# Eighteen small loads that nothing reads, in the queue of a decode block's cache loads

## The chip, the cores and the metric

The kernel runs on one core of a Trainium2 chip. The metric is the device time of one execution in microseconds (us). Three runs of the kernel before took 1303.91, 1304.32 and 1304.37 us; their median is 1304.32 us. One more execution was recorded by the profiler, and everything that is said here of single instructions and transfers comes from that one.

## The reference

The kernel computes one decode step of a transformer block for a batch of 2 sequences, one new token each, in float32. The width is 448. Attention has 16 heads of 256 numbers and a cache of 8192 keys and values for each head; behind it stands a gated network of width 1792 without a nonlinearity.

```python
def _A_ref(x, k_cache, v_cache, wq, wo):
    q = (x @ wq).reshape(B, Sq, H, Dh).transpose(0, 2, 1, 3)
    scores = jnp.einsum("bhqd,bhkd->bhqk", q, k_cache) * (Dh ** -0.5)
    p = _softmax(scores, axis=-1)
    o = jnp.einsum("bhqk,bhkd->bhqd", p, v_cache)
    return o.transpose(0, 2, 1, 3).reshape(B, Sq, H * Dh) @ wo

def _B_ref(x, w_gate, w_up, w_down):
    return ((x @ w_gate) * (x @ w_up)) @ w_down

h = x + _A_ref(_layernorm(x), k_cache, v_cache, wq, wo)
h2 = h + _B_ref(_layernorm(h), w_gate, w_up, w_down)
```

There are 32 pairs of a head and a sequence. Each has 8 MB of keys and 8 MB of values (8192 x 256 numbers of 4 bytes), so the two caches are 512 MB of the 561 MB that the kernel reads.

## The kernel before

A pair of a head and a sequence is called a query here; the loop `for i in range(NQ)` goes over the 32 of them. For each query two transfers are issued on SyncE's queue (SP), one behind the other in the program: `load_k` (L98) fetches its keys into a tile of 128 rows with 64 KB each, and `load_v` (L103) its values into another tile of the same size. Both tiles come from pools: the pool of K has one buffer, that of V has two.

With the keys, TensorE (PE) forms the scores in PSUM (L253). In every third query VectorE (DVE) first multiplies and adds half of the keys itself (L241, L245), and PE only sums its result (L259). DVE finds the maximum (L319), ScalarE (ACT) forms the exponentials `p` (L323), and DVE multiplies them with the values and adds up: in one pair of instructions for eight rows of blocks (L338, L339) or in eight single instructions (L342). After the loop come the weights `wo` (L351), gate, up and down (L358) on the same queue, and the matmuls of the output projection and of the gated network.

What sets the order: the schedule is by hand (`manual_schedule`), so each engine runs its instructions as the program writes them. SyncE issues one transfer after the other, and a transfer that has to wait holds all those behind it on SyncE. K of the next query waits until the last reader of the one K buffer is done (the scores, or DVE's part of them), and for the load that filled it before. V waits until the query before the last one has been read out of its buffer. Once issued, a transfer's rows lie in the rings of the 16 DMA engines, which work them off in order; SyncE goes on without waiting for them to land. There are eight semaphores for the completions of transfers (DMAHW0 to DMAHW7), used in turn.

The tile pool `const` (one buffer for each name) holds small tiles that live to the end, such as `oacc`, `nm` and `qd`.

Of the kernel before, what the change touches and what calls it, by code (L numbers as in the profile page):

```python
# [8 lines left out]
F32 = mybir.dt.float32  # L9
# [6 lines left out]
P = 128  # L16
# [4 lines left out]
GK = SK // G  # L21
# [38 lines left out]
def tile_decode_block(  # L60
# [24 lines left out]
    nc = tc.nc  # L85
    const = ctx.enter_context(tc.tile_pool(name="const", bufs=1))
# [9 lines left out]
    def load_k(b, h):  # L96
        t = kbuf.tile([P, 2, G, GK], F32, tag="k", align_bytes=512, name=f"k_{h}_{b}")
        nc.sync.dma_start(t.rearrange("p c g k -> p (c g k)"), kc[b, h])  # L98
        return t

    def load_v(b, h):
        t = vbuf.tile([P, NO, GK], F32, tag="v", align_bytes=512, name=f"v_{h}_{b}")
        nc.sync.dma_start(t.rearrange("p o k -> p (o k)"), vc[b, h])  # L103
        return t
# [62 lines left out]
    for rows, c, to in LAYOUT:  # L167
        k = rows.stop - rows.start
        n = c.stop - c.start
# [58 lines left out]
    def queries(h):  # L228
        q = one.tile([P, 2, B, R], F32, tag="q", name=f"q_{h}")
        nc.scalar.activation(  # L230
            q.rearrange("p c b r -> p (c b) r"),
            qT.rearrange("p k g j c b -> p (k g j) (c b)")[:, h, :, None]
            .to_broadcast([P, 2 * B, R]),
            AF.Copy,
        )
        return q

    def scores(s, q, i, kt):
        upper = kt[:, 1]
        if by_vector(i):  # L240
            nc.vector.tensor_scalar(  # L241
                upper[:, 0], upper[:, 0], qd[:, 0, i : i + 1], None, op0=ALU.mult
            )
            for o in range(1, G):
                nc.vector.scalar_tensor_tensor(  # L245
                    upper[:, 0], upper[:, o], qd[:, o, i : i + 1], upper[:, 0],
                    op0=ALU.mult, op1=ALU.add,
                )
        tiles = [slice(j * MM, (j + 1) * MM) for j in range(GK // MM)]
        for at in tiles:  # L250
            for c in range(1 if by_vector(i) else 2):
                for g in range(G):
                    nc.tensor.matmul(  # L253
                        s[g * R : (g + 1) * R, at], q[:, c, i % B, :], kt[:, c, g, at],
                        start=(c == 0), stop=(c == 1), skip_group_check=True,
                    )
        if by_vector(i):
            for at in tiles:
                nc.tensor.matmul(  # L259
                    s[:, at], block, upper[:, 0, at], start=False, stop=True,  # L260
                    skip_group_check=True,
                )

    def weights(a, z):

        n = z - a
        nmT = ps_m.tile([n, P], F32, tag="sm", name=f"nmT_{a}")
        nc.tensor.transpose(nmT, nm[:, a:z], ident)
        low = work.tile([n, 1], F32, tag="low", name=f"low_{a}")
        nc.vector.tensor_reduce(low, nmT, axis=AX.X, op=ALU.min)  # L270
        diag = work.tile([n, n], F32, tag="diag", name=f"diag_{a}")
        nc.vector.tensor_scalar(diag, ident[:n, :n], low, None, op0=ALU.mult)
        all_ps = ps_m.tile([P, n], F32, tag="sm", name=f"all_ps_{a}")
        nc.tensor.matmul(all_ps, ones[:n, :], diag, start=True, stop=True)
        w = work.tile([P, n], F32, tag="w", name=f"w_{a}")
        nc.vector.scalar_tensor_tensor(
            w, all_ps, float(R), nm[:, a:z], op0=ALU.mult, op1=ALU.subtract
        )
        nc.scalar.activation(w, w, AF.Exp)
        lw = work.tile([P, n], F32, tag="lw", name=f"lw_{a}")  # L280
        nc.vector.tensor_mul(lw, ls[:, a:z], w)
        l_ps = ps_m.tile([P, n], F32, tag="sm", name=f"l_ps_{a}")
        nc.tensor.matmul(l_ps, ones, lw, start=True, stop=True)
        rl = work.tile([P, n], F32, tag="rl", name=f"rl_{a}")
        nc.vector.reciprocal(rl, l_ps)
        nc.vector.tensor_mul(w, w, rl)
        return w

    def weigh(a, z, w):
        nc.vector.tensor_mul(  # L290
            oacc[:, a:z], oacc[:, a:z], w[:, :, None].to_broadcast([P, z - a, NO])
        )

    def turn(a, z):
        oT_ps = ps_m.tile([P, z - a, 2], F32, tag="sm", name=f"oT_ps_{a}")
        for r in range(G):
            nc.tensor.matmul(
                oT_ps[r * R : (r + 1) * R], gsum, oacc[:, a:z, r::G], start=True, stop=True
            )
        return oT_ps  # L300

    def heads_out(a, z, oT_ps):
        nc.vector.tensor_copy(
            oT[:, a // B : z // B].rearrange("p h c b -> p h b c"),
            oT_ps.rearrange("p (h b) c -> p h b c", b=B),
        )

    q_now = queries(0)

    for i in range(NQ):  # L310
        h, b = divmod(i, B)
        kt = load_k(b, h)
        vt = load_v(b, h)

        s = ps_s.tile([P, GK], F32, tag="s", name=f"s_{i}")
        scores(s, q_now, i, kt)
        if i == EARLY:
            oT_ps = turn(0, EARLY)
        nc.vector.tensor_reduce(nm[:, i : i + 1], s, axis=AX.X, op=ALU.max, negate=True)  # L319
        if i == EARLY:  # L320
            heads_out(0, EARLY, oT_ps)
        p = one.tile([P, GK], F32, tag="p", name=f"p_{i}")
        nc.scalar.activation(  # L323
            p, s, AF.Exp, bias=nm[:, i : i + 1], scale=1.0, accum_out=ls[:, i : i + 1]
        )

        if b == B - 1 and h + 1 < H:
            q_now = queries(h + 1)

        if i == EARLY - 1:  # L330
            w = weights(0, EARLY)
        if i == NQ - 1:
            w = weights(EARLY, NQ)

        n = WIDE[i % 3] if i < EARLY - B else 0
        if n:
            v = vt[:, :n, :]
            nc.vector.tensor_mul(v, v, p[:, None, :].to_broadcast([P, n, GK]))  # L338
            nc.vector.tensor_reduce(oacc[:, i, :n], v, axis=AX.X, op=ALU.add)  # L339
        for o in range(n, NO):  # L340
            v = vt[:, o, :]
            nc.vector.scalar_tensor_tensor(  # L342
                v, v, 1.0, p, op0=ALU.mult, op1=ALU.mult, accum_out=oacc[:, i, o : o + 1]
            )
        if i == EARLY - 1:
            weigh(0, EARLY, w)
# [26 lines left out]
    for c in range(DC):  # L373
        k = P if c < DC - 1 else HALF
# [32 lines left out]
    for m in range(DC + 1):  # L407
        at = min(m, DC - 1)
        rows = slice(0, P) if m < DC - 1 else slice((m - at) * HALF, (m - at + 1) * HALF)
        k = rows.stop - rows.start  # L410
# [11 lines left out]
    for rows, c, to in LAYOUT:  # L422
        k = rows.stop - rows.start
# [23 lines left out]
    for half in range(2):  # L447
        at = slice(half * 2 * P, (half + 1) * 2 * P)
        nc.vector.tensor_mul(hm[:, at], u_ps[:, at], g_sb[:, at])  # L449
    for half in range(2):  # L450
        for n in range(2):
            k = (2 * half + n) * P
# [81 lines left out]
```

## Time and profile before

| | |
|---|---|
| runs of the kernel | 1303.91, 1304.32, 1304.37 us; median 1304.32 us |
| the profiled execution | 1304.25 us, of which the span from first to last instruction is 1302.4 us |
| busy, share of the span | PE 26%, DVE 81%, ACT 6% |
| bytes read | 561.19 MB, 431 GB/s over the span |
| DMA packets | 11401, of which 1266 have under 512 bytes |
| granted TensorE clock, mean | 0.646 |

The busy time of an engine is the time in which one of its instructions runs. A DMA packet is one piece that one DMA engine moves in one go; a row of a tile of K or V is one packet of 65536 bytes. A completion, the write that tells a semaphore that a DMA engine has done its share of a transfer, is a packet of its own too, of 4 bytes. The view that lists stretches counts for its DMA columns the packets that start in the stretch: their whole time as a share of 16 engines, and their bytes. In a stretch of 10 ns with one packet in it, the share times 16 times 10 ns is that packet's time.

### The profile page before, as it was taken

The numbers are of one execution on the slowest core, as the hardware profiler recorded it, in microseconds if no ns is written. First come the engines' busy times: TensorE is split into PE (matmuls) and PEld (weight loads), VectorE is DVE, ScalarE is ACT, GpSimd is POOL, SyncE is SP. The second block draws the span as 40 slices with busy tenths as digits, with TensorE's granted clock in tenths as the row PEclk, the third lists the DMA queues.
The fourth block names the chain that finished last, engine by engine and source line by source line (L and its number), as shares of the span: only waits on it lengthen the run. The fifth ranks groups of instructions, "written<-read, shape, count | busy, mean of one in ns | idle before, by whom it ended". The sixth has DMA issues, their size and how long they took to land.

```text
span 1302.4 us, 5013 instructions
## 1 busy us (share of the span) xinstructions
PE 342.4 (26%) x2116; PEld 101.8 (8%) x2116; DVE 1061.1 (81%) x381; ACT 74.3 (6%) x89; POOL 1.4 (0%) x12
## 2 busy tenths in 40 slices
PE   2432112222212322211222211223211222221147
PEld 0100000000000000000000000000000000000012
DVE  1499879969987998899799889969987996967743
ACT  0100000000000000000000000000000000000000
POOL 0000000000000000000000000000000000000000
PEclk9766566676557666656766656676656667655769
DMA  9999999999999999999999999999999999999998
GB/s 419 419 449 421 447 423 443 427 443 427 441 429 439 427 441 427 439 431 437 427 437 427 439 431 435 436 433 437 431 439 431 439 429 439 429 442 425 445 414 354
DMA packets 11401, 561.50 MB, mean 431 GB/s; under 512 B 1266, under 2 KB 1524, under 8 KB 2420
## 3 DMA queue, kind: packets, MB, share of 16 engines
q1 hardware_dynamic: 11380, 561.20, 99.6%
q8 instruction: 16, 0.26, 0.1%
q14 instruction: 5, 0.04, 0.0%
HBM read 561.19 MB, written 0.00 MB: 431 GB/s over the span
## 4 chain that ended last, share of the span: by engine, by line
DMA 71%; PE 19%; DVE 9%; issue 1%; SPq 0%; ACT 0%; DVEq 0%
DMA k<-in_kc_dram 68%; PE s L253 15%; DVE k L245 6%; PE s L259 3%; DMA gu_t<-in_B_w_up_dram 3%; DVE v L342 2%; DVE k L241 1%; PE ff_ps L460 0%; PE u_ps L187 0%; SPq L358 0%; SPq L351 0%; PE ff_ps L453 0%; DVE tail L449 0%; SPq L107 0%; ACT tail L465 0%
## 5 line engine op out<-in xcount | busy, mean ns | idle before, releaser
L253 PE MATMUL s<-k,q 128*32 128x512 f32 x1696 | 255.5, 767 | 875.7 <-DMA k<-in_kc_dram 875.7
L338 DVE TENSOR_TENSOR v<-v,p 128x16384 f32<-128x16384 f32 x19 | 327.3, 17226 | 68.8 <-DMA v<-in_vc_dram 49.1
L339 DVE TENSOR_REDUCE oacc<-v 128x8 f32<-128x16384 f32 x19 | 327.2, 17220 | 0.7
L342 DVE SCALAR_TENSOR_TENSOR v<-v,p 128x2048 f32<-128x2048 f32 x104 | 231.1, 2288 | 33.9 <-ACT p L323 21.9
L253 PEld LDWEIGHTS s<-k,q 128*32 128x32 f32 x1696 | 68.8, 137 | 1059.4 <-issue 1059.4
L323 ACT ACTIVATE p<-s,nm 128x2048 f32<-128x2048 f32 x32 | 63.0, 1967 | 1128.6 <-DVE nm L319 1128.6
L319 DVE TENSOR_REDUCE nm<-s 128x1 f32<-128x2048 f32 x32 | 73.1, 2285 | 65.1 <-PE s L259 43.2
L245 DVE SCALAR_TENSOR_TENSOR k<-k,qd 128x2048 f32<-128x2048 f32 x33 | 77.6, 2352 | 1.2
L259 PE MATMUL s<-k,block 128*128 128x512 f32 x88 | 42.1, 622 | 33.5 <-DVE k L245 33.5
L241 DVE TENSOR_SCALAR k<-k,qd 128x2048 f32<-128x2048 f32 x11 | 14.2, 1287 | 13.1 <-DMA k<-in_kc_dram 11.0
L259 PEld LDWEIGHTS s<-k,block 128*128 128x128 f32 x88 | 16.4, 196 | 60.0 <-DVE k L245 39.9
L159 DVE COPY xT<-wq_t 128x8 f32<-128x8 f32 x1 | 0.2, 173 | 18.9 <-DMA wq_t<-in_wq_dram 18.9
L385 PE MATMUL acc_ps<-wo_t,oT 128*2 128x448 f32 x64 | 9.8, 712 | 11.8 <-DMA wo_t<-in_wo_dram 11.5
L187 PE MATMUL q_ps<-wq_t,xr 128*32 128x512 f32 x64 | 8.9, 704 | 1.3 <-DVE xr L172 1.0
L211 DVE COPY qT<-q_ps 128x32 f32<-128x32 f32 x2 | 0.4, 192 | 10.5 <-PE q_ps L208 10.5
L342 DVE DVE_READ_ACCUMULATOR v<-v,p 128x1 f32 x104 | 8.7, 83 | 0.0
L323 ACT ACTIVATION_READ_ACCUMULATOR p<-s,nm 128x1 f32 x32 | 6.2, 193 | 0.0
L142 PE MATMUL total_x<-sum_h_x,ones 128*128 128x2 f32 x2 | 0.6, 364 | 21.1 <-DVE sum_h_x L135 21.1
L449 DVE TENSOR_TENSOR tail<-u_ps,tail 128x256 f32<-128x256 f32 x2 | 0.8, 420 | 6.1 <-PE u_ps L187 6.1
L460 PE MATMUL ff_ps<-wd_t,hmT 128*2 128x224 f32 x28 | 5.5, 352 | 0.0
L460 PE MATMUL acc_ps<-wd_t,hmT 128*2 128x224 f32 x28 | 5.5, 352 | 0.0
L230 ACT ACTIVATE q<-qT 128x128 f32<-128x128 f32 x16 | 4.8, 297 | 0.0
(94 smaller groups left out, 58.9 us busy)
## 6 DMA issues: line engine op xcount, KB each, us to landing
wq_t<-in_wq_dram SPq DMA_DIRECT2D x1, 7172.0 KB, 19.7
wo_t<-in_wo_dram SPq DMA_DIRECT2D x1, 3584.0 KB, 17.8
wo_t<-in_wo_dram SPq DMA_DIRECT2D x1, 2688.0 KB, 23.8
gu_t<-in_B_w_gate_dram SPq DMA_DIRECT2D x1, 1792.0 KB, 29.2
gu_t<-in_B_w_up_dram SPq DMA_DIRECT2D x1, 1792.0 KB, 35.8
wd_t<-in_wd_dram SPq DMA_DIRECT2D x2, 896.0 KB, 17.2
gu_t<-in_B_w_gate_dram SPq DMA_DIRECT2D x1, 1344.0 KB, 32.0
wo_t<-in_wo_dram SPq DMA_DIRECT2D x1, 896.0 KB, 25.5
```

Source lines behind the costliest of these rows:

```text
L187: nc.tensor.matmul(ps[32 * g : 32 * g + 32, : wide[g]], xs.rearrange("p b r -> p (b r)"), w[:, at : at + wide[g]], start=(c == 0), stop=(c ...
L241: nc.vector.tensor_scalar(upper[:, 0], upper[:, 0], qd[:, 0, i : i + 1], None, op0=ALU.mult)
L245: nc.vector.scalar_tensor_tensor(upper[:, 0], upper[:, o], qd[:, o, i : i + 1], upper[:, 0], op0=ALU.mult, op1=ALU.add,)
L253: nc.tensor.matmul(s[g * R : (g + 1) * R, at], q[:, c, i % B, :], kt[:, c, g, at], start=(c == 0), stop=(c == 1), skip_group_check=True,)
L259: nc.tensor.matmul(s[:, at], block, upper[:, 0, at], start=False, stop=True, skip_group_check=True,)
L319: nc.vector.tensor_reduce(nm[:, i : i + 1], s, axis=AX.X, op=ALU.max, negate=True)
L323: nc.scalar.activation(p, s, AF.Exp, bias=nm[:, i : i + 1], scale=1.0, accum_out=ls[:, i : i + 1])
L338: nc.vector.tensor_mul(v, v, p[:, None, :].to_broadcast([P, n, GK]))
L339: nc.vector.tensor_reduce(oacc[:, i, :n], v, axis=AX.X, op=ALU.add)
L342: nc.vector.scalar_tensor_tensor(v, v, 1.0, p, op0=ALU.mult, op1=ALU.mult, accum_out=oacc[:, i, o : o + 1])
L385: nc.tensor.matmul(acc_ps[32 * j : 32 * j + B, :], oT[:, h, c, :], wo_t[:, k * D : (k + 1) * D], start=(h < 2 and j > 0), stop=(h >= H - 2 ...
L460: nc.tensor.matmul(ps, hmT[:, n, g, :], wd_t[:, k * D + a : k * D + a + YC], start=False, stop=(k == NF - 1), skip_group_check=True,)
```

## The change

A tile `scratch` of 80 bytes a row is added to the pool `const`. Behind V of queries 4 to 21 a load is issued, 18 in all, that copies a few bytes from the first V of the cache into `scratch`. Nothing reads `scratch`. Each of the 18 has another size: `rulers` gives the first row, the number of rows, the step between rows and the number of runs in a row; the size in numbers of 4 bytes is 2 more than its place in the list. All are issued by SyncE.

```diff
+    rulers = (
+        (0, 3, 1, 1), (64, 3, 1, 1), (0, 3, 4, 1), (0, 16, 1, 1), (0, 17, 1, 1), (0, 32, 1, 1),
+        (0, 48, 1, 1), (0, 64, 1, 1), (64, 64, 1, 1), (0, 96, 1, 1), (0, 112, 1, 1),
+        (16, 112, 1, 1), (0, 119, 1, 1), (0, 120, 1, 1), (0, 124, 1, 1), (0, 125, 1, 1),
+        (0, 8, 1, 2), (0, 3, 1, 2),
+    )
+    scratch = const.tile([P, 20], F32, name="scratch")
+
+    def load_ruler(n):
+        at, rows, step, runs = rulers[n]
+        size = 2 + n
+        to = scratch[at : at + (rows - 1) * step + 1 : step, :size]
+        src = vc[0, 0, at : at + (rows - 1) * step + 1 : step]
+        if runs == 1:
+            nc.sync.dma_start(to, src[:, :size])
+        else:
+            half = size // 2
+            to = scratch[at : at + rows, :20].rearrange(
+                "p (k z) -> p k z", k=2
+            )[:, :, :half]
+            src = src[:, : 2 * GK].rearrange("p (k z) -> p k z", k=2)[:, :, :half]
+            nc.sync.dma_start(to, src)
+
     q_now = queries(0)
 
     for i in range(NQ):
         h, b = divmod(i, B)
         kt = load_k(b, h)
         vt = load_v(b, h)
+        if 4 <= i < 22:
+            load_ruler(i - 4)
```

The instructions of PE, DVE, ACT and GpSimd keep their order; SyncE's queue gets 18 transfers more. The first place is where they begin, on SyncE from K of query 4 (`k_2_0`, head 2, sequence 0) on. Before:

```order
L98 DMA k_2_0_356<-in_kc_dram 128x16384 [waits DMAHW7_49,DVE_49,PE_49]
L103 DMA v_2_0_358<-in_vc_dram 128x16384 [waits DMAHW6_49]
L98 DMA k_2_1_398<-in_kc_dram 128x16384 [waits DMAHW1_49,PE_49]
L103 DMA v_2_1_400<-in_vc_dram 128x16384 [waits DMAHW0_49,DVE_49]
L98 DMA k_3_0_448<-in_kc_dram 128x16384 [waits DMAHW3_49,PE_49]
L103 DMA v_3_0_450<-in_vc_dram 128x16384 [waits DMAHW2_49,DVE_49]
```

The same stretch of SyncE's queue now; in brackets stand the semaphores that a transfer waits for.

```order
L98 DMA k_2_0_357<-in_kc_dram 128x16384 [waits DMAHW7_49,DVE_49,PE_49]
L103 DMA v_2_0_359<-in_vc_dram 128x16384 [waits DMAHW6_49]
L323 DMA scratch_192<-in_vc_dram 3x2
L98 DMA k_2_1_400<-in_kc_dram 128x16384 [waits DMAHW1_49,PE_49]
L103 DMA v_2_1_402<-in_vc_dram 128x16384 [waits DMAHW0_49,DVE_49]
L323 DMA scratch_192<-in_vc_dram 3x3
L98 DMA k_3_0_451<-in_kc_dram 128x16384 [waits DMAHW4_49,PE_49]
L103 DMA v_3_0_453<-in_vc_dram 128x16384 [waits DMAHW2_49,DVE_49]
L323 DMA scratch_192<-in_vc_dram 3x4 [waits DMAHW3_49]
```

Each small load stands between V of its query and K of the next one. The third waits for the completion of the first (DMAHW3), since both write row 0 of `scratch`; K and V wait for the same partners as before, whose semaphores have other numbers.

The second place is SyncE's queue from V of query 7 (`v_3_1`) on, where the load of 17 rows stands. Before:

```order
L103 DMA v_3_1_484<-in_vc_dram 128x16384 [waits DMAHW4_49]
L98 DMA k_4_0_526<-in_kc_dram 128x16384 [waits DMAHW7_49,PE_49]
L103 DMA v_4_0_528<-in_vc_dram 128x16384 [waits DMAHW6_49,DVE_49]
L98 DMA k_4_1_574<-in_kc_dram 128x16384 [waits DMAHW1_49,PE_49]
L103 DMA v_4_1_576<-in_vc_dram 128x16384 [waits DMAHW0_49,DVE_49]
```

Now:

```order
L103 DMA v_3_1_488<-in_vc_dram 128x16384 [waits DMAHW5_49]
L323 DMA scratch_192<-in_vc_dram 16x5 [waits DMAHW1_49]
L98 DMA k_4_0_531<-in_kc_dram 128x16384 [waits DMAHW2_49,PE_49]
L103 DMA v_4_0_533<-in_vc_dram 128x16384 [waits DMAHW6_49,DMAHW0_49,DVE_49]
L323 DMA scratch_192<-in_vc_dram 17x6 [waits DMAHW4_49]
L98 DMA k_4_1_580<-in_kc_dram 128x16384 [waits DMAHW5_49,PE_49]
L103 DMA v_4_1_582<-in_vc_dram 128x16384 [waits DMAHW3_49,DVE_49]
```

A small load here waits for the small load before it (the one of 17 rows for that of 16, DMAHW4). V of query 8 has one wait more: its semaphore, DMAHW6, was last used by the second small load, three queries earlier.

## Rows read from the trace of the kernel before

**Rows 1.** The page: span, DMA shares in 40 slices, packets, bytes, the chain's lines.

```profile
span 1302.4 us, 5013 instructions
...
DMA  9999999999999999999999999999999999999998
...
DMA packets 11401, 561.50 MB, mean 431 GB/s; under 512 B 1266, under 2 KB 1524, under 8 KB 2420
...
HBM read 561.19 MB, written 0.00 MB: 431 GB/s over the span
...
DMA k<-in_kc_dram 68%; PE s L253 15%; DVE k L245 6%; PE s L259 3%; DMA gu_t<-in_B_w_up_dram 3%; DVE v L342 2%; DVE k L241 1%; PE ff_ps L460 0%; PE u_ps L187 0%; SPq L358 0%; SPq L351 0%; PE ff_ps L453 0%; DVE tail L449 0%; SPq L107 0%; ACT tail L465 0%
```

**Rows 2.** The chain in order of time: start us, us, what.

```profile
633.06 26.27 DMA k<-in_kc_dram
...
659.46 8.48 PE s L253 x64
667.96 30.02 DMA k<-in_kc_dram
...
707.76 28.84 DMA k<-in_kc_dram
...
1253.03 37.48 DMA gu_t<-in_B_w_up_dram
1290.55 1.05 PE u_ps L187 x6
```

**Rows 3.** SyncE's issues, 620 to 720 us: start us, us, what.

```profile
633.06 0.33 SPq L98 DMA_DIRECT2D k<-in_kc_dram  x1
633.44 0.42 SPq L103 DMA_DIRECT2D v<-in_vc_dram  x1
667.96 0.33 SPq L98 DMA_DIRECT2D k<-in_kc_dram  x1
674.62 0.33 SPq L103 DMA_DIRECT2D v<-in_vc_dram  x1
707.76 0.33 SPq L98 DMA_DIRECT2D k<-in_kc_dram  x1
713.48 0.33 SPq L103 DMA_DIRECT2D v<-in_vc_dram  x1
```

**Rows 4.** The tile v: its costliest form (min/median/max ns), issue to landing.

```profile
L342 DVE SCALAR_TENSOR_TENSOR v<-v,p x104: 2284/2289/2294, 137.8 to 1275.2; 128x2048 f32<-128x2048 f32 x104
...
DMA to landing us min/median/max: 42.3/42.8/58.3
```

**Rows 5.** Stretches, most of 10 ns with one DMA packet.

```profile
core 0: us, PE busy (x) PEld busy (x) DVE busy (x) ACT busy (x) POOL busy (x), PEclk, DMA share, GB/s
660.12:660.13 0.01, 0.01 (x4) 0.00 (x0) 0.01 (x1) 0.00 (x0) 0.00 (x0) 0.50 15.11 6554
1298.74:1298.75 0.01, 0.01 (x4) 0.00 (x0) 0.00 (x0) 0.00 (x0) 0.00 (x0) 1.00 0.46 179
676.59:676.60 0.01, 0.00 (x0) 0.00 (x0) 0.01 (x1) 0.00 (x0) 0.00 (x0) 0.50 0.06 0
316.77:316.78 0.01, 0.01 (x8) 0.01 (x3) 0.01 (x1) 0.00 (x0) 0.00 (x0) 1.00 5.92 1638
317.70:317.71 0.01, 0.01 (x4) 0.00 (x0) 0.01 (x1) 0.00 (x0) 0.00 (x0) 1.00 18.12 6554
600.00:1240.00 640.00, 149.26 (x893) 43.18 (x893) 540.15 (x194) 36.53 (x43) 0.00 (x0) 0.63 1.00 434
```

**Rows 6.** DMA packets of four stretches: 38.6:39.6, 1236.5:1238.4, 1238.4:1239.2, 1239.2:1240.2.

```profile
DMA packets 32, 1.05 MB, mean 1049 GB/s; under 512 B 16, under 2 KB 16, under 8 KB 16
...
DMA packets 25, 1.05 MB, mean 552 GB/s; under 512 B 9, under 2 KB 9, under 8 KB 9
...
DMA packets 2, 0.13 MB, mean 164 GB/s; under 512 B 0, under 2 KB 0, under 8 KB 0
...
DMA packets 19, 0.79 MB, mean 786 GB/s; under 512 B 7, under 2 KB 7, under 8 KB 7
```

## The prediction

> **What bounds the kernel now.** I read the page first: the DMA engines are at 9 tenths or more in 39 of 40 slices, and the chain of work that ended last is 68% waiting for K [rows 1]. Then the chain in order of time. K lands at 633.06 + 26.27 = 659.33, at 667.96 + 30.02 = 697.98 and at 707.76 + 28.84 = 736.60: one query every 38.64 us [rows 2]. A row of K or V is one packet of 65536 bytes, and it takes 15.11 x 16 x 10 ns = 2.418 us [rows 5]. A query has 256 of them, 16 for each of the 16 rings, and 16 x 2.418 = 38.69 us. So in mid-run a ring does nothing but such packets, one behind the other, and from 600 to 1240 us the share is 1.00 at 434 GB/s [rows 5].
>
> SyncE's issues show why no ring runs dry: K is issued at 707.76 while V, issued at 674.62, lands only 42.8 us later, at 717.4 [rows 3, 4]. K's issue waits for the scores, but the data are 8 to 10 us behind the queue. What an engine saves is worth nothing, and what a ring gets to do in addition comes on top, unless that ring had a lead.
>
> Some rings have one. The 16 completions of the first K lie within 1 us (38.6 to 39.6); those of the last K fall into 9 up to 1238.4, none up to 1239.2, and 7 after that [rows 6]. The seven late rings set the end, the nine others are roughly 1 to 3 us ahead. At the end the chain goes through the last transfer of `up`, 37.48 us, into the last matmuls [rows 2], so a late ring delays the end by its whole lag.
>
> **The change, part by part.** Nothing is removed. Added are 18 loads with 1080 rows or runs in all (1058 rows in the sixteen with one run, 2 x 8 and 2 x 3 in the other two).
>
> Bytes: under 60 KB in all, which at 434 GB/s is 0.14 us. I count it in the packets.
>
> SyncE: an issue takes 0.33 to 0.42 us [rows 3]. The small load stands behind V. V at 674.62 is issued by 674.95, and the small load before it lies behind the V of 633.44, which lands 42.8 us later at 676.2 [rows 3, 4]. So SyncE waits there 1 to 4 us (the rings that end last included) and issues the small load before about 680. What is queued behind it is K of the next query, and that isn't ready before 707.76. The cover is 27 us, and the cost nothing; were it gone, K's data still would not be missed for another 8. The extra wait of V of query 8 is for a load of three queries before: nothing.
>
> SBUF: `scratch` takes 80 bytes a row, and other tiles may move. DVE's instruction on V takes 2284 to 2294 ns in both V buffers [rows 4], so its place doesn't matter: nothing.
>
> Rings: this is the term. Each row is a small packet, and each ring that takes part adds a completion. No packet of 8 to 76 bytes stands in the trace, so I bound its price. Below: a completion of 4 bytes takes 0.06 x 16 x 10 ns = 9.6 ns [rows 5]. Above: a packet of 1792 bytes takes 0.46 x 16 x 10 ns = 74 ns, of which 66 ns are its bytes at the rate of the large ones (65536 bytes in 2418 ns), so 8 ns are left for the packet itself [rows 5]. By both rows a tiny packet costs about 9.6 ns; by size it is far nearer to the completion, and I take that. A boundary between two transfers is free by the first paragraph: K and V leave no gap in 38.64 us.
>
> How many fall on one ring? The 79 loads over 128 rows and the store of two rows give 79 x 16 + 2 = 1266 packets under 512 bytes, just what the page has [rows 1]. So 128 rows go to 16 rings, and two rows to two. Spread as evenly as can be, the busiest ring gets 75 of the 1080 packets; all on one, 1080. If the rings that take part must get equal shares, as those two cases have it, 17 rows can only go to one ring, 119 to 7 with 17 each, 124 to 4 with 31 each, 125 to 5 with 25 each, and if every load begins at the same ring, this one gets 139, the next two 122 and the fourth 117. I take this one, since both rows have equal shares. The sum for the first ring is (139 + 18) x 9.6 ns = 1.5 us; with an even spread it is (75 + 18) x 9.6 = 0.9 us. One or the other of these four loaded rings may be ahead at the end. With 7 of 16 rings late, and those within 1 us of each other (1239.2 to 1240.2 holds them), it is likely that one of the four is among the late, but not that it is the last; I take 0.4 us off. Forecast: +1.1 us. The profiled execution took 1304.25 us, 0.07 below the median of 1304.32, so the sum goes on the median: 1305.4 us.
>
> On the shares, the Trainium skill's page "DMA: Bandwidth & Descriptors" (Why a DMA increments its semaphore by 16 and not by 1) says that a transfer uses the largest number of engines up to 16 that divides its row count, the lowest-numbered ones. The trace agrees for 128 and 2 rows; no run here shows the others. By that rule the sum would be the 1.5 us, without it 0.9.
>
> **The rivals.**
>
> *A floor under every packet.* A ring could need a fixed time for any packet that has to be read from HBM, up to the 74 ns of the smallest such packet in the trace. For it: the completion, which carries the low price, is no copy of a cache row. Against it: the 8 ns that 1792 bytes need beyond their rate. Then (75 x 74 + 18 x 9.6) = 5.7 us with an even spread, 1310.0, and 139 x 74 + 0.2 = 10.5 us with equal shares, 1314.8; less up to 3 us where the loaded rings were ahead. It decides from (2.6 + 0.4 - 0.2) us / 139 = 20 ns a packet on. The same page of the Trainium skill (Specifications) says that below 512 bytes a DMA engine does a read-modify-write; it states no price, and no row here shows such a write into SBUF.
>
> *Each small load breaks the stream.* An instruction fetch of 16384 bytes on another queue takes 5.92 x 0.16 = 0.95 us, and the packet behind it 18.12 x 0.16 = 2.90 instead of 2.42 [rows 5]: 1.43 us for bytes that are worth 0.60. If every small load on the first ring cost these 0.82 us, the sum would be 18 x 0.82 = 14.8 us, 1319.1. Against it: that fetch comes from another queue, and the boundaries between K and V on this one cost nothing.
>
> *All rows of a load on one ring*, always the same: 1080 x 9.6 = 10.4 us, 1314.7. Against it stand the 16 and 2 completions.
>
> *Hidden altogether, or gained.* If the four loaded rings are all among the nine early ones, the lag stays within their lead: 1304.3. For a gain there is only that SBUF addresses and the rings' leads shift by chance; a gain of more than 2.6 us has no mechanism that I can name.
>
> **How the numbers follow.** Of a change under 0.2%, 2.6 us, a measurement of this kernel can hardly tell that it is there. Forecast with a completion's price, whichever way the rows are shared, together with the hidden case: 0.66, all of it within 0.2%; its own range is 1303.9 (the lowest run before) to 1306.9. Floor 0.20, broken stream 0.08, one ring 0.04: these 0.32 are slower. A gain 0.02. The range of 8 in 10 begins at 1303.9 and takes in of the floor's 1307 to 1314.8 the part up to 1312.5, about two thirds: 0.65 + 0.14 = 0.79.
>
> **What would show it.** On the page after: 1080 small packets more and their completions, the share of the DMA engines in mid-run still 1.00, SyncE's small loads issued 1 to 4 us behind V and K still issued when the scores end. The price: stretches of 10 ns around a small packet with a share of about 0.06, and 0.46 if the floor holds. The shares: the number of completions of each small load, one for that of 17 rows if shares must be equal. K's landings should stay 38.64 us apart but for a few tenths where 17, 31 or 25 packets lie on one ring; a step of 0.8 us at each small load would mean the broken stream, and steps that grow with the rows would mean a dear packet. The forecast is wrong if the small packets fill more than 2.6 us of the last ring, or if SyncE reaches K later than the scores end.

## The result

The changed kernel takes 1306.12 us (median of 20 runs, 1305.9 to 1310.47), against 1304.33 us of the kernel before on the same chip (20 runs). The medians are 1.8 us apart; the ratio is 1.0016, with a 95% interval of 1.0009 to 1.0022 (1.2 to 2.9 us). The forecast was 1305.4 us in a range of 1303.9 to 1312.5, no difference beyond 0.2%. The median lies within that bound, and the interval shows that a small loss is real; the cost was put at 1.1 us and is 1.8.

The span of the kernel after is 1304.4 us, 2.0 longer than before. The row of its packets answers to [rows 1].

```profile
DMA packets 12661, 561.56 MB, mean 431 GB/s; under 512 B 2526, under 2 KB 2784, under 8 KB 3680
```

The row tells how the small loads were shared. There are 2526 - 1266 = 1260 small packets more: the 1080 rows and 180 completions. If each load goes to the largest number of rings up to 16 that divides its rows, the 18 loads have 3 + 3 + 3 + 16 + 1 + 7 x 16 + 7 + 15 + 4 + 5 + 8 + 3 = 180 of them (7 x 16 for 32 to 112 rows). It fits to the packet.

The chain of waits of the kernel after (start us, us, what) answers to [rows 2].

```profile
699.65 9.83 PE s L253 x64
...
750.67 26.42 DMA k<-in_kc_dram
...
785.84 30.35 DMA k<-in_kc_dram
...
867.12 26.27 DMA k<-in_kc_dram
...
1098.84 26.37 DMA k<-in_kc_dram
...
1133.98 30.82 DMA k<-in_kc_dram
...
1254.85 37.51 DMA gu_t<-in_B_w_up_dram
```

Three landings of K in the kernel before, to set beside them:

```profile
865.86 26.28 DMA k<-in_kc_dram
...
1097.85 26.66 DMA k<-in_kc_dram
...
1134.36 28.75 DMA k<-in_kc_dram
```

The last small load is issued at 835.71 us. K that landed at 865.86 + 26.28 = 892.14 before lands at 893.39 now, 1.25 us later, and the last transfer of `up` lands at 1292.36 instead of 1253.03 + 37.48 = 1290.51, 1.85 us later. So most of the lag is gathered in the loop, while the small loads pass. One step can be seen singly: from 750.67 + 26.42 = 777.09 to 785.84 + 30.35 = 816.19 there are 39.10 us, not 38.64; the load of 125 rows lies between (five rings, 25 packets each).

The lag doesn't stay the same behind the loop. It is 0.70 us at the landing of 1098.84 + 26.37 = 1125.21 (1124.51 before) and 1.69 at that of 1164.80 (1163.11 before), with no small load in between. In this stretch a large packet takes 18.47 x 0.16 = 2.96 us, right behind an instruction fetch of 8192 bytes:

```profile
1149.32:1149.33 0.01, 0.00 (x0) 0.00 (x0) 0.01 (x3) 0.00 (x0) 0.00 (x0) 0.50 18.47 6554
```

The kernel before has such a fetch at the same place (1149.07 us), and its K lands 38.60 us after the last one all the same. So it seems that which ring such a fetch meets can move the end of an execution by up to 1 us, beside what the small loads do.

SyncE's issues in the kernel after answer to [rows 3], and behind them stands a row of what SyncE's queue waited for (us in total, times, longest).

```profile
680.33 0.35 SPq L323 DMA_DIRECT2D scratch<-in_vc_dram  x1
709.50 0.34 SPq L98 DMA_DIRECT2D k<-in_kc_dram  x1
```

```profile
SPq L323 <- DMA scratch<-in_vc_dram: 51.0, 12, 6.3
```

SyncE waits in front of a small load for 51.0 / 12 = 4.3 us on average, at most 6.3. The small load is issued at 680.33, and K at 709.50, right when the scores end (699.65 + 9.83 = 709.48). The wait is covered.

What a small packet costs its ring is seen in stretches of the kernel after, with the columns of [rows 5]. The first holds the 31 packets of the load of 124 rows on one ring (64 bytes each); the second, the large packet behind them; the third, one behind 25 packets of 68 bytes (the load of 125 rows); the fourth, one behind 17 packets of 56 bytes (119 rows), with two small packets in the stretch; the fifth, the large packet behind the 17 packets of 24 bytes that the load of 17 rows put on its one ring.

```profile
756.57:756.80 0.23, 0.00 (x0) 0.00 (x0) 0.00 (x0) 0.00 (x0) 0.00 (x0) 0.50 0.10 9
...
756.80:756.81 0.01, 0.00 (x0) 0.00 (x0) 0.00 (x0) 0.00 (x0) 0.00 (x0) 0.50 17.86 6554
...
796.11:796.12 0.01, 0.00 (x0) 0.00 (x0) 0.00 (x0) 0.01 (x1) 0.00 (x0) 0.50 17.10 6554
...
677.47:677.48 0.01, 0.00 (x0) 0.00 (x0) 0.01 (x1) 0.00 (x0) 0.00 (x0) 0.50 16.92 6565
...
368.50:368.51 0.01, 0.00 (x0) 0.00 (x0) 0.00 (x0) 0.01 (x1) 0.00 (x0) 0.50 15.11 6554
```

Counting the packets of 756.5 to 756.8 gives 33 (31 and two completions):

```profile
DMA packets 33, 0.00 MB, mean 7 GB/s; under 512 B 33, under 2 KB 33, under 8 KB 33
```

The 31 packets and two completions take 0.23 us, so one starts every 7 ns; this is called a packet's slot below. The times that their records give are longer, 0.10 x 16 x 0.23 us / 33 = 11 ns each, and overlap. The large packet behind them takes 17.86 x 0.16 = 2.86 us instead of 2.42. That is 0.23 + 0.44 = 0.67 us, 20 ns for each of the 33. Behind 25 packets of 68 bytes the large one takes 17.10 x 0.16 = 2.74 us, 0.32 more; behind 17 of 56 bytes 2.69 (16.92 x 0.16 = 2.71, less the two small records), 0.27 more. The 17 packets of 24 bytes have no such effect, called a tail below: the packet behind them takes 15.11 x 0.16 = 2.42 us. So with the same number of packets, 17, the bytes decide whether there is a tail. The completion's 9.6 ns, which the forecast took, is more than a tiny packet's own slot, and less than what it costs when a long row of them holds up what follows.

### The profile page after: what moved, and what is told of

Same layout as the page of the kernel before. It is cut to its first block, busy times and chain, and to the rows that moved or that the text cites. A ratio compares the mean times of both kernels' runs of the same rounds, so it can differ in the third digit from the quotient of the medians.

```text
span 1304.4 us, 5033 instructions
## 1 busy us (share of the span) xinstructions
PE 351.3 (27%) x2116; PEld 104.7 (8%) x2116; DVE 1061.1 (81%) x381; ACT 74.3 (6%) x89; POOL 1.4 (0%) x12
## 2 busy tenths in 40 slices
DMA packets 12661, 561.56 MB, mean 431 GB/s; under 512 B 2526, under 2 KB 2784, under 8 KB 3680
## 4 chain that ended last, share of the span: by engine, by line
DMA 70%; PE 19%; DVE 10%; issue 1%; SPq 0%; ACT 0%; DVEq 0%
DMA k<-in_kc_dram 67%; PE s L253 15%; DVE k L245 6%; PE s L259 4%; DMA gu_t<-in_B_w_up_dram 3%; DVE v L368 3%; DVE k L241 1%; PE ff_ps L486 0%; PE u_ps L187 0%; SPq L384 0%; SPq L377 0%; PE ff_ps L479 0%; DVE tail L475 0%; SPq L107 0%; ACT tail L491 0%
## 5 line engine op out<-in xcount | busy, mean ns | idle before, releaser
L259 PE MATMUL s<-k,block 128*128 128x512 f32 x88 | 50.9, 733 | 28.4 <-DVE k L245 28.4
L241 DVE TENSOR_SCALAR k<-k,qd 128x2048 f32<-128x2048 f32 x11 | 14.1, 1286 | 13.1 <-DMA k<-in_kc_dram 9.0
L259 PEld LDWEIGHTS s<-k,block 128*128 128x128 f32 x88 | 19.3, 229 | 61.0 <-DVE k L245 34.6
L411 PE MATMUL acc_ps<-wo_t,oT 128*2 128x448 f32 x64 | 9.9, 724 | 11.4 <-DMA wo_t<-in_wo_dram 11.2
L211 DVE COPY qT<-q_ps 128x32 f32<-128x32 f32 x2 | 0.4, 192 | 11.4 <-PE q_ps L208 11.4
```

The lines of the kernel that those rows point to most:

```text
L241: nc.vector.tensor_scalar(upper[:, 0], upper[:, 0], qd[:, 0, i : i + 1], None, op0=ALU.mult)
L259: nc.tensor.matmul(s[:, at], block, upper[:, 0, at], start=False, stop=True, skip_group_check=True,)
L411: nc.tensor.matmul(acc_ps[32 * j : 32 * j + B, :], oT[:, h, c, :], wo_t[:, k * D : (k + 1) * D], start=(h < 2 and j > 0), stop=(h >= H - 2 ...
```

## The experiments

All are edits of the changed kernel, and each difference is taken from the median of the kernel before, timed beside it. The small loads write bytes that nothing reads, so none of them changes what the kernel computes.

**All loads on 128 rows.**

```diff
-    rulers = ( ... )
+    rulers = ((0, 128, 1, 1),) * 18
```

> All 18 small loads have 128 rows, so each of the 16 rings gets 8 of them from each load, 144 in all, and no ring has a lead that could hide it. Theory A (equal shares over the largest number of rings that divides the row count; a tiny packet costs its ring about 18 ns, 9 to 12 ns of its own record and the rest on the large packet behind it, as the 2.3 us that the loaded rings of the changed kernel are later by and their 117 to 139 packets have it): 144 x 18 ns = 2.6 us over before, about 1307.0. Theory B (the forecast's price, 9.6 ns each and nothing behind it): 144 x 9.6 ns + 18 completions = 1.6 us, 1305.9. Theory C (each load breaks the stream, whatever its rows): as much as the changed kernel, +1.8 us, 1306.1.

Measured: 1306.12 us, before 1304.24: +1.9 us, ratio 1.0015 (1.0006 to 1.0023). Each ring has 144 packets and 18 completions, so 1.88 us / 162 = 11.6 ns each; between theory A and B. It is no help against C, which gives the same time here.

**All loads on 127 rows.**

```diff
-    rulers = ( ... )
+    rulers = ((0, 127, 1, 1),) * 18
```

> One row less in each of the 18 loads: 127 instead of 128. Theory A: 127 has no divisor from 2 to 16, so all 127 rows of each load go to one ring, 18 x 127 = 2286 packets on it; at 18 ns that is 41 us, less up to 3 us if that ring had a lead: 1342 to 1346. At theory B's 9.6 ns: 22 us, 1323 to 1326. A theory with an even spread of rows (8 a ring, 7 on one): the same as with 128 rows, 1306 to 1307. Theory C: +1.8 us, 1306.1.

Measured: 1334.49 us, +30.3 us, ratio 1.0234 (1.022 to 1.0248). One row fewer costs 28 us more. The packets' row of its page:

```profile
DMA packets 13705, 561.60 MB, mean 421 GB/s; under 512 B 3570, under 2 KB 3828, under 8 KB 4724
```

3570 - 1266 = 2304 = 18 x 127 + 18: each load has one completion, so all its rows went to one ring. An even spread and theory C both fall. Over 2304 packets 30.25 us would be 13.1 ns each, between A and B, but the trace shows that the time is not lost packet by packet on that ring. These rows show SyncE's issue of K, the packets that start from 251.6 to 254.4 us, and the stretch behind them:

```profile
244.43 9.37 SPq L98 DMA_DIRECT2D k<-in_kc_dram  x1
...
DMA packets 144, 0.00 MB, mean 1 GB/s; under 512 B 144, under 2 KB 144, under 8 KB 144
...
254.50:255.50 1.00, 0.00 (x0) 0.00 (x0) 1.00 (x1) 0.00 (x0) 0.00 (x0) 0.50 1.91 655
```

K stands behind a small load here, and its issue takes SyncE 9.37 us instead of 0.33: SyncE does not go on at once here. It ends at 253.80, while the small packets pass. It is so in all 18 queries (4.9 to 10.3 us); in the run with 128 rows K's issue took 0.33 to 0.41 us each time. For 2.8 us no ring starts a large packet, more than the 2.42 that one takes: all 16 rings have run dry. The 144 packets are the 127 rows, their completion and the 16 of V; V is worked off, and K is not there yet. When K comes, 655 KB start in one us, ten large packets on ten rings, and they take 1.91 x 16 = 30.6 us, 3.06 us each instead of 2.42. Of the 30.25 / 18 = 1.68 us that a query loses, these longer first packets are 0.64; by difference, an estimate, the dry time is the other 1.04. So this run gives no price of a packet, and neither A nor B has what happened in it. Why K's issue is held behind 127 rows on one ring is not shown.

**All loads on 3 rows.**

```diff
-    rulers = ( ... )
+    rulers = ((0, 3, 1, 1),) * 18
```

> All 18 small loads have 3 rows: one tiny packet and one completion on each of three rings, 18 each. Theory A: 18 x (18 + 10) ns = 0.5 us on rings that are mostly ahead, so 0 to 0.5 us, 1304.3 to 1304.8. Theory B: 0 to 0.35 us. Theory C: each load costs what it cost in the changed kernel, +1.8 us, 1306.1.

Measured: 1304.44 us, +0.2 us, ratio 1.0004 (0.9995 to 1.0012). With the same number of loads, C expected 1.8. A load as such costs nothing that this can measure. These packets fall on three rings only, which might have a lead; the two runs below with 8 and 76 bytes have no ring without small packets, and they tell C from the others again.

**Each load twice.**

```diff
-    scratch = const.tile([P, 20], F32, name="scratch")
-
-    def load_ruler(n):
+    scratch = const.tile([P, 32], F32, name="scratch")
+
+    def load_ruler(n, first, wide):
...
-        size = 2 + n
-        to = scratch[at : at + (rows - 1) * step + 1 : step, :size]
+        size = min(2 + n, wide)
+        to = scratch[at : at + (rows - 1) * step + 1 : step, first : first + size]
...
-            to = scratch[at : at + rows, :20].rearrange(
+            to = scratch[at : at + rows, first : first + wide].rearrange(
...
-            load_ruler(i - 4)
+            load_ruler(i - 4, 0, 20)
+            load_ruler(i - 4, 20, 12)
```

> Each small load of the change is issued twice, the second time with at most 12 numbers a row and into other columns, so that it doesn't wait for the first. Theory A: the loaded rings get twice their lag, 2 x 2.3 = 4.6 us; the first 0.5 to 0.7 us are hidden by the lead of that ring, so +4.0 us, 1308.3. Theory B: twice 1.1 to 1.5 us less the same lead, +2.2 us, 1306.5. If only rows of many bytes cost more than their record: between the two, about 1307.3. Theory C: +3.6 us, 1307.9.

Measured: 1308.20 us, +4.0 us, ratio 1.0041 (1.0027 to 1.0054), as A has it. Twice the loads cost 3.96 us, once 1.79, a little more than twice. If the first part of a lag is hidden by a lead, 2L - h = 3.96 and L - h = 1.79 give a lag L of 2.2 us and a lead h of 0.4 us; that is no more than an estimate. It takes the second set to cost what the first does, though its rows have 48 bytes at most, and each median has a few tenths of scatter. C's 3.6 is near as well, but has fallen above.

**The source rows close together.** To see where the held-up packets come from, the 127 rows and the change's own rows were read from one row of V, 512 bytes apart.

```diff
-        src = vc[0, 0, at : at + (rows - 1) * step + 1 : step]
+        near = vc[0, 0, 0].rearrange("(p z) -> p z", z=P)
+        src = near[at : at + (rows - 1) * step + 1 : step]
...
-            src = src[:, : 2 * GK].rearrange("p (k z) -> p k z", k=2)[:, :, :half]
+            src = src[:, :P].rearrange("p (k z) -> p k z", k=2)[:, :, :half]
```

With 127 rows in all loads:

> 18 loads of 127 rows again, all on one ring, but their source rows lie 512 bytes apart inside one row of V instead of 65536 bytes apart. With 65536 bytes between them the run took 30 us more, 13 ns a packet, of which only about 7 ns lie between one tiny packet and the next and the rest on the large packet behind them. Theory D (the rest comes from the source addresses, which meet in one place of the memory): the rest goes, 2286 x 7 ns = 16 us less a lead of up to 3 us, 1317 to 1320. Theory E (it comes from the packets themselves, wherever they read): no difference, 1334.

Measured: 1335.32 us, +31.1 us, ratio 1.0238 (1.0224 to 1.0252). With the rows of the change:

> The 18 small loads of the change with their source rows 512 bytes apart inside one row of V instead of 65536 bytes. Theory D: the loaded rings lose 117 to 139 packets x 7 ns = 0.8 to 1.0 us instead of 2.3 us, of which 0.7 us are hidden by their lead, so 1304.5 to 1304.8. Theory E: as the changed kernel, 1306.1.

Measured: 1306.06 us, +1.8 us, ratio 1.0015 (1.0007 to 1.0024). Theory D fails here, where it had 1304.5 to 1304.8: the addresses that the rows come from do not matter. The run with 127 rows doesn't decide it, since K's issue is held there too (4.9 to 10.2 us in each of the 18 queries), and the dry rings make its time.

**Only the loads that fall on few rings, and only the others.**

```diff
-        if 4 <= i < 22:
+        if 4 <= i < 22 and i - 4 in (4, 12, 14, 15):
```

> Only the four small loads whose rows fall on few rings: 17, 119, 124 and 125 rows (one, seven, four and five rings with 17, 17, 31 and 25 packets each). Theory A: the four most loaded rings are later by 73 to 90 x 18 ns = 1.3 to 1.6 us, less their lead of 0.7 us: +0.6 to 0.9 us, 1304.9 to 1305.2. With an even spread these four would be 26 packets a ring, +0.4 us. Theory C (a load costs 0.1 us whatever its rows): +0.4 us.

Measured: 1305.69 us, +1.5 us, ratio 1.0011 (1.0003 to 1.002). More than A had for it, and more than the 0.4 of an even spread or of C, which lies at the lower end of the interval. With `not in` instead of `in`:

> The other fourteen small loads without those four: at most 49 packets on a ring, 42 on nearly all. Theory A: 42 to 49 x 13 to 18 ns = 0.5 to 0.9 us, and the ring that ends last gets them too, so no lead hides them: 1304.8 to 1305.2. Theory C: fourteen eighteenths of 1.8 us, +1.4 us, 1305.7.

Measured: 1305.02 us, +0.8 us, ratio 1.0004 (0.9995 to 1.0013); inside A's span, with an interval that doesn't exclude zero. So by the medians four loads of 385 rows cost more than fourteen with 695, though the two intervals overlap. The two parts sum to 2.3 us, 0.5 more than both together; A would have them sum to 1.8. Each interval is some 1.2 us wide to either side, so this difference is not told apart from scatter.

**Bytes of a row.** All loads on 128 rows, with 8 bytes each, and with 76.

```diff
-        size = 2 + n
+        size = 2
```

> 18 loads of 128 rows, all with 8 bytes a row. Theory F (a tiny packet costs its ring more, the more bytes it has: about 5 ns at 8 bytes and 17 ns at 76, as the landings of K grew from 38.67 to 38.78 us apart in the run where 128 rows had 8 to 76 bytes): 18 x 9 x 5 ns = 0.8 us, 1305.0. Theory G (13 ns whatever the bytes): +1.9 us, 1306.1.

Measured: 1305.36 us, +1.0 us, ratio 1.0006 (0.9998 to 1.0015).

```diff
-        size = 2 + n
+        size = 19
```

> 18 loads of 128 rows, all with 76 bytes a row. Theory F: 18 x 9 x 17 ns = 2.8 us, 1307.0. Theory G: +1.9 us, 1306.1.

Measured: 1306.51 us, +2.2 us, ratio 1.0014 (1.0005 to 1.0023). Over 162 packets and completions of a ring these are 6.2 and 13.3 ns. The order is F's, the spread smaller than F had it (5 and 17); the two intervals overlap, while the runs themselves (1305.26 to 1306.4, and 1306.21 to 1306.64) hardly do. C would have both runs at the same time.

**A wait without cover.** The loads of 3 rows, each issued a second time into the same bytes.

```diff
-    rulers = ( ... )
+    rulers = ((0, 3, 1, 1),) * 18
...
             load_ruler(i - 4)
+            load_ruler(i - 4)
```

> 18 loads of 3 rows, and behind each one the same load once more into the same bytes, so that it waits for the first on SyncE's queue, in front of K of the next query. By the issues and landings of before, the first lands with V, about 8 to 10 us after the scores have freed the buffer of K. Theory H (what is queued behind a waiting transfer waits too): K is issued only when V has landed, all rings run dry for the time from issue to first packet, 1.5 to 2 us with the two issues, in each of 18 queries: 27 to 36 us, 1331 to 1340. Theory I (SyncE's waits are covered anyway, as the single loads' wait is): as the 3 rows alone, 1304.5.

Measured: 1353.72 us, +49.4 us, ratio 1.0376 (1.036 to 1.0392). H holds, and its size was too low. SyncE's issues in that kernel:

```profile
712.44 0.38 SPq L103 DMA_DIRECT2D v<-in_vc_dram  x1
712.86 40.38 SPq L318 DMA_DIRECT2D scratch<-in_vc_dram  x2
753.34 0.35 SPq L98 DMA_DIRECT2D k<-in_kc_dram  x1
753.79 0.38 SPq L103 DMA_DIRECT2D v<-in_vc_dram  x1
```

and its packets from 751.5 to 754 us:

```profile
DMA packets 28, 0.00 MB, mean 0 GB/s; under 512 B 28, under 2 KB 28, under 8 KB 28
```

Between the two small loads of a query SyncE waits 40 us, K is issued only at 753.34, and for 2.5 us no ring starts a large packet. The period is 753.79 - 712.44 = 41.35 us instead of 38.64: 2.7 us in each of 18 queries, 49 us.

## Why the prediction was right, and where its size was off

The bound. The kernel after is still at the rate of its rings, and K's issue follows the scores as before. That a ring's added packets come on top is shown by the run with 128 rows and by the doubled loads.

SyncE. Predicted to cost nothing, with a wait of 1 to 4 us and 27 us of cover. The wait was 4.3 us on average and 6.3 at most, and K left when the scores ended. The step holds; the run with the wait in front of K shows what stood behind the cover. Here the prediction was too mild: it said that K's data would not be missed for 8 us, but a wait that lasts until V lands uses up all of that, and then the 2.5 us come in full. The runs with 127 rows show a second way to the same loss, which the prediction did not have: there SyncE waits for nothing, but the issue of K itself takes up to 10 us.

The shares. The forecast took equal shares on as many rings as divide the rows; the counts of 180 completions, and of 18 with 127 rows, show them. The Trainium skill's page "DMA: Bandwidth & Descriptors" (Why a DMA increments its semaphore by 16 and not by 1) says the same; the trace now agrees for 17 to 127 rows too. That it is always the lowest-numbered rings, no row here names.

The price. This is the term that was mis-sized: 9.6 ns a packet, the completion's. In the change 1.79 us over the 157 packets and completions of the first ring are 11.4 ns even if no lead hid anything, and 11.6 in the run with 128 rows, where every ring gets the same. The packet's own slot is less than was forecast, 7 ns. What was missed is the large packet behind, which no row of before could show: the sum took it to cost nothing. Put together from the rows above, the first ring gets 157 x 7 ns = 1.1 us of slots and tails of 0.44, 0.32 and 0.27 us behind its rows of 31, 25 and 17 packets, 2.1 us in all instead of 1.5, near the lag of 2.2 worked out from the doubled loads. It is an estimate: the rows don't name their ring, and shorter rows are counted without a tail.

The lead. It was put at 0.4 us, and 2.1 or 2.2 less the measured 1.79 leaves 0.3 to 0.4. That it fits so well is partly luck: it rests on one pair of medians, and in the profiled execution the lag of K's landings moved between 0.70 and 1.69 us behind the last small load. That execution took 1306.14 us, much like the median, so a part of the median's 1.8 us may come from where the instruction fetches fall; no run separates that part.

The rivals. A floor of 74 ns would have made the 144 packets a ring in the run with 128 rows 10.7 us; they took 1.9, and one of 64 bytes starts every 7 ns. The broken stream fell with the loads of 3 rows (+0.2 us, where 18 x 0.82 = 14.8 were its price). All rows on one ring is true of 17 and of 127 rows, and not of the others. Hidden altogether is excluded by the interval.

What stays open is why a large packet takes longer behind a row of small ones, and why K's issue is held when 127 rows lie on one ring in front of it. Where the rows are read from is excluded for the first. Whether it lies with the writes into SBUF was not tried.

## What to carry to other kernels

Where the rings are the bound, count for every transfer on how many of them it falls and how many packets the busiest one gets; a row count that no number from 2 to 16 divides puts all rows on one ring. 18 loads of 127 rows cost 30 us, of 128 rows 2, and what cost so much was not the small packets but the next large transfer, whose issue was held until the rings had run dry. So look at the time that an issue takes, too. Small loads behind a long stream that are spread over the rings cost by the packet, some 6 to 14 ns here in the mean, not by the load. A wait on the issuing queue is free only as long as what stands behind it isn't due: two small loads into the same bytes, one behind the other, cost 49 us where single ones cost 0.2.

## What the runs showed of the hardware

Small packets of 64 bytes started every 7 ns on a ring, while the record of each lasted 11 ns. They cost up to 20 ns each all the same: the rest appeared on the large packet behind them, 2.86 us instead of 2.42 behind 31 packets of 64 bytes and 2.69 behind 17 of 56 bytes, while 17 packets of 24 bytes left no trace. With 128 rows over all rings the cost grew with the bytes by the medians, 6.2 ns at 8 and 13.3 ns at 76 bytes a packet.

With a load of 127 rows on one ring in front of it, the issue of the next K took SyncE 4.9 to 10.3 us instead of 0.33, all 16 rings ran dry, and ten first packets of K that started together took 3.06 us each instead of 2.42.
